# Recurrence in two slots a unit, with one feed-forward round between slots, on one core

## The chip, the cores and the metric

One NeuronCore of a Trainium2 chip runs the whole program. TensorE (PE) multiplies into PSUM, which has eight banks of 512 fp32 columns; VectorE (DVE) and ScalarE (ACT) take the results out of PSUM; GpSimd (POOL) does elementwise work on SBUF; SyncE (SP) issues DMAs. Each engine works through its own instructions in a fixed order and waits on semaphores. The metric is the device time of one execution in microseconds, the median of several runs.

## The reference, cut to what matters

```python
# r, k, v, w, a, b: (batch 4, heads 8, seq 768, dim 40)
for t in range(S):
    y[:, :, t] = einsum('bhd,bhde->bhe', r_t, state)
    Sa = einsum('bhde,bhe->bhd', state, a_t)
    state = state * w_t[:, :, None, :] - einsum('bhd,bhe->bhde', Sa, b_t)
    state = state + einsum('bhd,bhe->bhde', v_t, k_t)
x = y.transpose(0, 2, 1, 3).reshape(3072, 320)
h = x @ w_in                      # 320 -> 2048
g = h * clip(h + 3, 0, 6) / 6
out = g @ w_out                   # 2048 -> 320
```

A recurrence over 768 steps with a 40x40 state for each of 32 heads, then a feed-forward block over its 3072 output rows.

## The kernel before

**Units.** The sequence is cut into 12 blocks of 64 steps. A unit is one block of two batch entries: 24 units (`NK`), in 6 groups of four (`NU`). Within a unit the recurrence is turned into matrix products. What does not need the state is prepared ahead (`prepare`, stages W, gam, A, B, F, factor, K, E, EV): transposes of the inputs, decays by two scans on DVE (lines 541 and 552), score products of 64x64, and EV, a product with V. F of four units together gives a triangular matrix that DVE inverts (`invert`): some 60 small multiply and add instructions one after another (lines 738 and 744), then two stream transposes, tb and tt (lines 747 and 752). Two products on PE (`third_block`, lines 773 and 796) with four ACT copies after each finish the inverse, for two units at a time. What needs the state (`step`, stages RT, VT, R, C, S, U, UT, rS, sn, H, y, move, move2) follows unit by unit: R reads the state, U and UT need R (added to EV by DVE, line 857) and the inverse, H needs UT, y needs the masked H, and sn adds into the state. The moves are DMAs that lay y out as the feed-forward's input.

**Products in quarters.** Recurrence products use the array in four quarters, 64x64 each, and write pairs of PSUM banks: `ps_pair` deals a pair, and several products of up to 512 columns together share one. The weights of UT, rS and y are taken 64 columns wide (`SLOT`) although the data is 40 wide (`D`).

**Feed-forward.** Each unit has two rounds. A round is `expand` (32 full 128x128 matmul instructions as the trace counts them, line 1051, and 16 that are 64 rows deep, the `narrow` part), an ACT relu and a DVE multiply (lines 1066 and 1067) for each of two banks, and `contract` (16 instructions 320 columns wide, line 1092), which runs one round later. `feed_forward` is a generator that gives this in pieces: four pieces of `expand` and eight of `contract`.

**Order.** Everything is in an order written out by hand. The first two groups have tables of their own (lines 1131 to 1303), and after them 18 turns of inversion steps and 1.25 pieces of feed-forward each. From line 1307 on, each unit of the recurrence is cut into four blocks (`BLOCKS`); in each block `a_block` runs the stages of the unit in hand, then those of a unit four to six ahead, each as a run of products by `together`, and between those runs `feed` deals some 1.4 to 3.1 pieces of feed-forward with, while an inversion is open, two or three of its steps a piece. The recurrence ends well before the feed-forward: the last stretch is feed-forward alone.

**PSUM.** Two `pair` tiles and two one-bank `h` tiles for the feed-forward's hidden sums, one bank `one` for whole transposes and one, `o`, for the output.

The part of `together` by which a run's products come first and its results after the whole run:

```python
                rest = stage()
                next(rest)
                begun.append((name, rest))
```

Of the kernel before, what the change touches and what calls it, by code (L numbers as in the profile page):

```python
# [30 lines left out]
def kernel(  # L31
# [68 lines left out]
    lent = tc.tile_pool(name="lent", bufs=1, space=PSUM)  # L100
    pools = {"lent": lent.__enter__(), "pair": ps}
    pairs = deque([("pair", 2), ("pair", 2), ("lent", 1)])

    def pair():

        pairs.rotate(-1)
        tag, bufs = pairs[-1]
        return pools[tag].tile([P, 2, 512], F32, name=tag, tag=tag, bufs=bufs)

    def begun_ffn():  # L110

        lent.__exit__(None, None, None)
        pairs.clear()
        pairs.append(("pair", 2))
        pools["h"] = ctx.enter_context(tc.tile_pool(name="hidden", bufs=1, space=PSUM))


    def ps_any(shape):
        tag, bufs = ring[0]
        ring.rotate(-1)  # L120
        at = 0
        if tag == "whole":
            t = pair()
            open_half[0] = None
        elif tag != "pair":
            t = bank(tag, [P, 512], bufs)
        elif open_half[0] is None:
            t = open_half[0] = pair()
        else:
            t, at = open_half[0], 512  # L130
            open_half[0] = None
        views, step = [], 1
        for d in reversed(shape[1:]):
            views.insert(0, [step, d])
            step *= d
        return _ap(t[:], at, views)
# [3 lines left out]
    def ps_pair(*dims):  # L140
# [4 lines left out]
        if shared[0] is None or shared[1] + n > 512:  # L145
            shared[:] = pair(), 0
            open_half[0] = None
        at = shared[1]
# [5 lines left out]
        t = shared[0][:]  # L154
# [53 lines left out]
    nc.vector.memset(start[:], 0.0)  # L208
    nc.vector.memset(start[:].rearrange("p (n i) -> p n i", i=HB + 1)[:, :, 0:1], 1.0)
# [216 lines left out]
    PE, DONE = 1, 2  # L426
# [94 lines left out]
    def prepare(i, F):  # L521
        n, o = i % NU, data[i]
        halves = i >= 2 * NU
        def w_stage():
# [14 lines left out]
            fetch("W", following(i))  # L539
            prods = o["prods"] = tmp.tile([P, NB, 2, HB + 1], F32, name="prods", bufs=2)  # L540
# [5 lines left out]
        def gam_stage():  # L546
# [14 lines left out]
            def copy(to, x):  # L561
                if i < NU:
# [12 lines left out]
            if NU <= i <= 2 * NU:  # L575
                fetch("V", i)
# [57 lines left out]
        def factor_stage():  # L634
# [29 lines left out]
            if i > 2 * NU:  # L664
                fetch("V", i)
# [3 lines left out]
        def k_stage():  # L669
            x = turn_pairs(o["KN"])  # L670
            yield PE
            kt = o["kt"] = turned("kt")
            nc.vector.tensor_tensor(out=kt[:], in0=x[:], in1=o["rg"][:], op=ALU.mult)
# [143 lines left out]
    def step(i):  # L817
# [52 lines left out]
        def s_S():  # L870
# [10 lines left out]
            new_U()  # L881

        def s_U():

            if fresh:
                new_U()
# [16 lines left out]
        def s_UT():  # L903

            up = ps_pair(2, P)
            for j in range(2):
                for s in range(2):
                    for x in range(2):
                        for rs in range(2):
                            pr = 2 * j + rs  # L910
                            nc.tensor.matmul(out=up[x][half(rs), j, half(x ^ s)],
                                             lhsT=RR[half(x), s, pr * D:pr * D + SLOT],
# [7 lines left out]
        def s_rS():  # L920

            ysp = ps_pair(2, 2, BL)
            for j in range(2):
                for q in range(2):
                    for s in range(2):
                        for rs in range(2):
                            nc.tensor.matmul(out=ysp[rs][half(s), j, q, :],  # L927
                                             lhsT=m["S"][half(rs, D), q, j, half(s)],
# [32 lines left out]
        def s_y():  # L961
            y = ps_pair(NPR, BL)
            for name in "KB":
                for pr in range(NPR):
                    j, rs = pr // 2, pr % 2
                    for s in range(2):
                        for q in range(2):
                            h = 2 * pr + s
                            nc.tensor.matmul(  # L969
                                out=y[q][half(s), pr, :],  # L970
                                lhsT=o[name][half(q), h * D:h * D + SLOT],
# [44 lines left out]
    narrow, spread, LATEST = [], [False], 2  # L1016
# [7 lines left out]
    def feed_forward():  # L1024

        last = None
        while True:
# [7 lines left out]
            yield from expand(ready[i], r * NQ, gts)  # L1035
# [9 lines left out]
    def expand(xt, j0, gts):  # L1045

        hp = [pools["h"].tile([P, NQ, P], F32, name="h", tag="h", bufs=2) for _ in range(2)]
        begun = [0, 0]

        def add(c, i, lhsT, rhs):  # L1050
            nc.tensor.matmul(out=hp[c][:, i, :], lhsT=lhsT, rhs=rhs, start=(begun[c] == 0),  # L1051
# [11 lines left out]
        def results():  # L1063
            for c in range(2):
                gt = ffn.tile([P, NQ, P], F32, name="gt", bufs=5)
                nc.scalar.activation(out=gt[:], in_=hp[c][:], func=AF.Relu, bias=three[:], scale=1.0)  # L1066
                nc.vector.scalar_tensor_tensor(out=gt[:], in0=gt[:], scalar=6.0, in1=hp[c][:],  # L1067
                                               op0=ALU.min, op1=ALU.mult)
                gts.append(gt)

        narrow.append(short)
        for c in range(2):
# [53 lines left out]
    def pieces(n):  # L1126

        owed[0] += n * (8 / 9 if spread[0] else 1)
# [20 lines left out]
    def run(stage, steps=0, mixed=0, deals=0):  # L1149

        for at in stage:
            if at == DONE:
                return
            aside(steps, mixed)
            deal(deals)

# [143 lines left out]
    for _ in range(18):  # L1300
        aside(3)
        pieces(1.25)
    aside(3 * L)

    OWN_STAGES = [["RT", "VT"], ["R", "C", "S"], ["U", "UT", "rS"], ["sn", "H"], ["y"],
                  ["move", "move2"]]
    AHEAD_STAGES = [["W", "gam"], ["A", "B"], ["F", "K"], ["E", "factor"], ["EV"]]  # L1310
    CLOSE_STAGES = [["W", "gam"], ["A", "B"], ["F", "K", "factor"], ["E"], ["EV"]]


    PRODUCTS = ["W", "S", "K", "RT", "VT", "A", "B", "factor",
                "y", "EV", "R", "C", "U", "UT", "rS", "sn", "H", "E", "F"]
    RESULTS = ["RT", "y", "W", "VT", "EV", "R", "S", "C", "A", "B", "move", "move2",
               "U", "UT", "rS", "F", "K", "sn", "H", "E", "factor", "gam"]
    TURNS = PRODUCTS[:3]
    WIDTH = {"R": NPR * D, "U": NPR * D, "sn": NPR * D, "EV": NPR * D}
    BLOCKS = 4  # L1320
    FIRST_NARROW = PRODUCTS[len(TURNS)]

    def together(stages):

        begun, banks = [], 0

        def finish():
            begun.sort(key=lambda x: RESULTS.index(x[0]))
            for _, rest in begun:
                for _ in rest:  # L1330
                    pass
            begun.clear()
            shared[0] = open_half[0] = None
            ring.clear()
            ring.extend(TURNS_IN)

        for name in PRODUCTS:
            if name == FIRST_NARROW and narrow and spread[0] and stages:
                narrow[0]()
            for stage in stages.get(name, []):  # L1340
                if name in TURNS:
                    need = 2 * (open_half[0] is None) if ring[0][0] == "pair" else 1
                else:
                    width = WIDTH.get(name, NPR * BL)
                    need = 2 * (shared[0] is None or shared[1] + width > 512)
                if banks + need > 5:
                    finish()
                    banks, need = 0, 1 if name in TURNS else 2
                banks += need
                rest = stage()  # L1350
                next(rest)
                begun.append((name, rest))
        begun.extend((name, stage()) for name in stages if name not in PRODUCTS
                     for stage in stages[name])
        finish()

    begins = {u: max(3 * (u - 2 * NU), BLOCKS * (u - NU - AHEAD)) for u in range(2 * NU, NK)}
    coming, ahead, own = deque(range(2 * NU, NK)), {}, {}

    def a_block(m):  # L1360

        if coming and begins[coming[0]] == m:
            u = coming.popleft()
            close = coming and begins[coming[0]] < m + BLOCKS
            ahead[u, m] = prepared(u), CLOSE_STAGES if close else AHEAD_STAGES
        if m % BLOCKS == 0 and m // BLOCKS + NU < NK:
            i = m // BLOCKS + NU
            own[i, m] = step(i), OWN_STAGES
        parts = {}, {}
        for (u, begin), (fs, order) in sorted(own.items()) + sorted(ahead.items()):  # L1370
            if m - begin < len(order):
                for name in order[m - begin]:
                    parts[begin % BLOCKS > 0].setdefault(name, []).append(fs[name])
        for k, part in enumerate(parts):
            together(part)
            if any(u % NU == NU - 1 and m - begin == 2 and k == (begin % BLOCKS > 0)
                   for u, begin in ahead):
                third.clear()
                side.append(invert(group_F[-1], third))
            yield  # L1380

    def feed(n, inversion):

        whole = int(n)
        for k in range(whole):
            pieces(1)
            aside(inversion)
        pieces(n - whole)

    m = 0  # L1390
    for i in range(NU, NK):
        spread[0] = i >= 2 * NU - 1
        for j in range(BLOCKS):
            rate, inversion = 3.5, 0
            if i + AHEAD >= NK + NU - 1:
                rate = 4.5
            if i < 2 * NU - 1:
                rate = 2.8
            parts = a_block(m)
            next(parts)  # L1400
            if side or i % NU == NU - 1 and rate < 4:

                rate, inversion = 6.2, 2 + (i < 2 * NU)
            feed(rate / 2, inversion)
            for _ in parts:
                pass
            if i % NU < 2 and j < 2:
                if i % NU == 0:
# [43 lines left out]
```

## Time and profile before

| what | value |
|---|---|
| median of 3 runs | 799.55 us (799.53 to 800.25) |
| span of the profiled execution | 798.4 us |
| PE busy | 727.1 us, 91% |
| DVE busy | 501.3 us, 63% |
| ACT busy | 307.2 us, 38% |
| POOL busy | 176.3 us, 22% |
| PE busy in 300:700 | 398.5 of 400 us |
| PE busy in 0:140 | 81.4 of 140 us |

The profile is of one execution. Its tables give, for each group of instructions, the line of the kernel, the engine, what is written from what, the shape and the count, then total and mean time, then the engine's idle time just before them and what ended it. A matmul of fp32 stands in the trace as two instructions. Timelines give start, length, and the count of a merged run. Since matmuls are pipelined, the price of a run is read from its start to the next run's start.

### The profile page before, as it was taken

Reading aid. Unit: us, or ns where it says so; the run is one execution under the profiler, and the core shown is the slowest. Engines: PE = TensorE matmul, PEld = TensorE weight load, DVE = VectorE, ACT = ScalarE, POOL = GpSimd, SP = SyncE. Lnnn points to the kernel's source line nnn. Section 1 sums busy time; section 2 is a strip of 40 time slices with the busy share of each in tenths; the row PEclk is TensorE's granted clock in tenths of the full one; section 3 lists DMA queues with packets and bytes.
Section 4 is the critical chain, followed back from the end, with each engine's and each line's share of the span. In section 5 each row is a group of like instructions: output and inputs, shape, how many; then the busy total and the mean of one; then the engine's idle time right before and its main releaser. Section 6 shows DMA issues by size and latency. Waiting matters only on the chain.

```text
span 798.4 us, 35294 instructions
## 1 busy us (share of the span) xinstructions
PE 727.1 (91%) x15832; PEld 617.9 (77%) x15832; DVE 501.3 (63%) x986; ACT 307.2 (38%) x648; POOL 176.3 (22%) x318
## 2 busy tenths in 40 slices
PE   5624676999999989999999999999999999999998
PEld 4624575878778878888888888888888888888886
DVE  8889787679555699455698445898444983322210
ACT  2336653321654424453344453324444324412111
POOL 6403012420322222223124123304122202000000
PEclk9855888999999999999999999999999999999999
DMA  9484563420224321233222233213222101110000
GB/s 122 88 183 111 143 169 56 76 50 9 49 52 68 64 51 31 50 64 56 44 43 43 44 59 64 46 33 58 44 51 46 24 17 30 30 25 13 14 19 17
DMA packets 174214, 45.02 MB, mean 56 GB/s; under 512 B 157424, under 2 KB 172784, under 8 KB 174064
## 3 DMA queue, kind: packets, MB, share of 16 engines
q1 hardware_dynamic: 169760, 42.03, 27.6%
q8 instruction: 125, 2.05, 1.1%
q10 hardware_dynamic: 4304, 0.74, 0.6%
q14 instruction: 25, 0.20, 0.1%
HBM read 34.08 MB, written 3.93 MB: 48 GB/s over the span
## 4 chain that ended last, share of the span: by engine, by line
PE 73%; DVE 13%; issue 5%; SPq 3%; DMA 3%; ACT 2%; POOL 1%; DVEq 0%; POOLq 0%; ACTq 0%
PE h L1051 25%; PE o L1092 22%; PE pair L509 4%; PE pair L969 3%; PE pair L946 2%; DVE prod L738 2%; DVE x L744 2%; PE pair L481 2%; PE one L471 2%; SPq L455 2%; PE pair L853 2%; PE pair L891 2%; DVE prods L541 1%; PE pair L927 1%; DVE wm L552 1%
## 5 line engine op out<-in xcount | busy, mean ns | idle before, releaser
L1051 PE MATMUL h<-xt,win 128*128 128x128 f32 (+1 forms) x2304 | 251.3, 283 | 2.7 <-DVE gt L1067 2.7
L1051 PEld LDWEIGHTS h<-xt,win 128*128 128x128 f32 (+1 forms) x2304 | 231.8, 193 | 19.8 <-issue 4.4
L1092 PE MATMUL o<-wout,gt 128*128 128x320 f32 x768 | 229.6, 442 | 0.0
L1092 PEld LDWEIGHTS o<-wout,gt 128*128 128x128 f32 x768 | 138.1, 190 | 50.4 <-issue 0.2
L1067 DVE SCALAR_TENSOR_TENSOR gt<-gt,h 128x512 f32<-128x512 f32 x96 | 62.0, 681 | 70.5 <-ACT gt L1066 70.5
L1066 ACT ACTIVATE gt<-h,three 128x512 f32<-128x512 f32 x96 | 62.2, 686 | 99.7 <-PE h L1051 99.3
L981 POOL TENSOR_TENSOR yg<-ys,gam 128x512 f32<-128x512 f32 x22 | 39.0, 1772 | 160.3 <-DVE ys L980 73.7
L738 DVE TENSOR_TENSOR prod<-x 128x30 f32<-128x30 f32 (+9 forms) x180 | 67.1, 373 | 8.8 <-POOL x L723 3.3
L660 POOL TENSOR_TENSOR KBt<-K,rgt 128x320 f32<-128x320 f32 x22 | 19.0, 865 | 212.6 <-ACT rgt L649 197.2
L744 DVE TENSOR_TENSOR x<-x,prod 128x30 f32<-128x30 f32 (+9 forms) x180 | 62.2, 345 | 5.4
L954 DVE TENSOR_TENSOR state<-pair,state 40x320 f32<-40x320 f32 (+1 forms) x44 | 21.4, 487 | 65.4 <-PE pair L946 39.1
L517 DVE COPY_PREDICATED score<-mask,pair 128x512 f32<-128x512 int32 x71 | 50.0, 723 | 1.0 <-PE pair L509 0.5
L980 DVE TENSOR_TENSOR ys<-pair,ys 128x512 f32<-128x512 f32 x22 | 15.2, 690 | 40.8 <-PE pair L687 21.8
L552 DVE TENSOR_TENSOR_SCAN wm<-wm,start 128x528 f32<-128x528 f32 x24 | 37.8, 1574 | 0.8
L541 DVE TENSOR_TENSOR_SCAN prods<-wm,start 128x528 f32<-128x528 f32 x24 | 30.8, 1288 | 10.1 <-ACT wm L538 10.0
L831 ACT ACTIVATE RT<-pair 128x512 f32<-128x512 f32 x21 | 12.5, 597 | 52.8 <-PE pair L481 52.8
L692 ACT ACTIVATE EV<-pair 64x320 f32<-64x320 f32 x44 | 19.0, 432 | 32.9 <-PE pair L687 22.3
L806 ACT ACTIVATE tinv<-pair 32x256 f32<-32x256 f32 x48 | 18.0, 375 | 30.8 <-PE pair L796 30.1
L569 POOL COPY gam<-prods 128x256 f32<-128x256 f32 x24 | 22.5, 938 | 31.4 <-DVE prods L541 30.6
L969 PE MATMUL pair<-score,KBt 64*64 64x64 f32 x1472 | 27.8, 224 | 1.2 <-DVE state L954 1.2
L1110 ACT ACTIVATE ob<-o 128x320 f32<-128x320 f32 x22 | 9.6, 435 | 49.0 <-PE o L1092 24.8
L969 PEld LDWEIGHTS pair<-score,KBt 64*64 64x64 f32 x1472 | 24.5, 137 | 3.8 <-DVE state L954 1.8
(262 smaller groups left out, 1049.0 us busy)
## 6 DMA issues: line engine op xcount, KB each, us to landing
V<-in_v_dram SPq DMA_DIRECT2D x96, 40.0 KB
out_dram<-ob SPq DMA_DIRECT2D x47, 80.0 KB
R<-in_r_dram SPq DMA_DIRECT2D x92, 40.0 KB
B<-in_b_dram SPq DMA_DIRECT2D x42, 80.0 KB
K<-in_k_dram SPq DMA_DIRECT2D x42, 80.0 KB
W<-in_w_dram SPq DMA_DIRECT2D x37, 80.0 KB
A<-in_a_dram SPq DMA_DIRECT2D x37, 80.0 KB
xt<-yg SPq DMA_DIRECT2D x72, 40.0 KB
```

The costliest lines, as they stand in the source:

```text
L509: nc.tensor.matmul(out=o[i][half(q), n, :], lhsT=lhs[half(i, D), n ^ (2 * q * swap), half(q)], rhs=rhs[half(i, D), n, half(q)], start=True ...
L517: nc.vector.copy_predicated(out=x[:].rearrange("p (i h) t -> p i h t", i=2), mask=mask8, data=o[2])
L541: nc.vector.tensor_tensor_scan(out=prods[:].rearrange("p r m i -> p (r m i)"), data0=wm[:, 0:SCAN], data1=start[:], initial=0.0, op0=ALU.m ...
L552: nc.vector.tensor_tensor_scan(out=back, data0=back, data1=start[:], initial=0.0, op0=ALU.mult, op1=ALU.add)
L738: nc.vector.tensor_tensor(out=pv, in0=_ap(x[:], (i + 1) * L + i, [[L, n], [0, i]]), in1=_ap(x[:], i * L, [[0, n], [1, i]]), op=ALU.mult,)
L744: nc.vector.tensor_tensor(out=rest, in0=rest, in1=pv, op=ALU.add)
L969: nc.tensor.matmul(out=y[q][half(s), pr, :], lhsT=o[name][half(q), h * D:h * D + SLOT], rhs=m[name][half(q), 4 * rs + 2 * s + j, :], start ...
L981: nc.gpsimd.tensor_tensor(out=yg[:], in0=m["ys"][:].rearrange("p r q t -> p r (q t)"), in1=o["G"][:], op=ALU.mult)
L1051: nc.tensor.matmul(out=hp[c][:, i, :], lhsT=lhsT, rhs=rhs, start=(begun[c] == 0), stop=(begun[c] == 3 * NQ - 1))
L1066: nc.scalar.activation(out=gt[:], in_=hp[c][:], func=AF.Relu, bias=three[:], scale=1.0)
L1067: nc.vector.scalar_tensor_tensor(out=gt[:], in0=gt[:], scalar=6.0, in1=hp[c][:], op0=ALU.min, op1=ALU.mult)
L1092: nc.tensor.matmul(out=op[:], lhsT=gts[c][:, n, :], rhs=wout[:, c * HJ + r * NQ + n, :], start=((split or r == 0) and c == 0 and n == 0), ...
```

## The change

The steady part, from the second group's recurrence and the third group's preparation on, is ordered anew. Each unit has two slots. The even slot of unit i holds, of the units in hand, RT and VT of unit i and rS, sn, H, y of unit i-1, and of unit i+4 the stages F, E and factor. The odd slot holds R, C, S, U, UT of unit i, W, gam, A, B, K of unit i+5, and EV of unit i+4. A slot's products stand in one run, with results taken between them (`both`), and the `narrow` part of the next round of feed-forward ends the run. Between two slots stands a `window`: one whole round (expand and the contract of the round before), and two rounds in every eighth slot. A window in which no unit is ready for the feed-forward is empty. Inversion steps go two to a piece into the windows, four to a piece in the first two.

PSUM pairs become three fixed tiles, given out by longest free; `expand` takes one of them for its hidden sums. The six banks are written once by PE at the start. UT, rS and y take weights of 40 columns. K is transposed in halves like A and B, and two copies of `gam_stage` move from DVE to ACT for units from the third group on. The 18 turns of filler ahead of the steady part are gone.

```diff
+    pairs = [[ps.tile([P, 2, 512], F32, name=f"pair{i}"), i] for i in range(3)]
     def pair():
-        pairs.rotate(-1)
-        tag, bufs = pairs[-1]
-        return pools[tag].tile([P, 2, 512], F32, name=tag, tag=tag, bufs=bufs)
+        x = min(pairs, key=lambda x: x[1])
+        clock[0] += 1
+        x[1] = HELD + clock[0]
+        taken.append(x)
+        return x[0]
...
     nc.vector.memset(start[:], 0.0)
+    for x in pairs:
+        for c in range(2):
+            nc.tensor.matmul(out=x[0][:, c, :], lhsT=start[:, 0:P], rhs=start[:, 0:512], start=True, stop=True)
     nc.vector.memset(start[:].rearrange("p (n i) -> p n i", i=HB + 1)[:, :, 0:1], 1.0)
...
             def copy(to, x):
-                if i < NU:
+                if i < NU or halves:
                     nc.scalar.activation(out=to, in_=x, func=AF.Copy)
...
         def k_stage():
-            x = turn_pairs(o["KN"])
+            x = turn_in(o["KN"], halves)
...
-                            nc.tensor.matmul(out=up[x][half(rs), j, half(x ^ s)],
-                                             lhsT=RR[half(x), s, pr * D:pr * D + SLOT],
+                            nc.tensor.matmul(out=up[x][half(rs, D), j, half(x ^ s)],
+                                             lhsT=RR[half(x), s, pr * D:pr * D + D],
...
-                                lhsT=o[name][half(q), h * D:h * D + SLOT],
+                                lhsT=o[name][half(q), h * D:h * D + D],
...
-    for _ in range(18):
-        aside(3)
-        pieces(1.25)
-    aside(3 * L)
...
+        results("move", "move2")
+        if s % 2:
+            products("W")
+            results("W", once=True)
+            both("R", "EV")
+            both("C")
+            results("W")
+            both("U", "UT")
+            products("A", "B")
+            products("K")
+            if narrow:
+                narrow[0]()
+            both("S")
+            results("gam", "A", "B", "K")
+        else:
+            both("F")
+            both("H", "E")
+            both("rS", "sn")
+            both("y")
+            both("RT", "VT")
+            both("factor")
+            if narrow:
+                narrow[0]()
...
+    for s in range(begins(2 * NU), 2 * NK + 2):
+        if s == begins(2 * NU):
+            spread[0] = True
+            while next(stream) != OPEN:
+                pass
+            lends_hidden()
+        slot(s)
+        window(s, 2 if s % (2 * NU) == 2 * NU - 1 and s > 2 * NU else 1)
```

`both(names)` writes the products of the named stages and then at once the instructions that take their results; `products` and `results` do the one or the other. `window` draws pieces of feed-forward until the next round opens, and in the first and third slot of a group it also runs the two `third_block`s: their first product after the sixth piece, or at the end where there are fewer, and the second at the end.

## The prediction

> **What bounds the kernel now.** I read the page's busy times and slices first, then the timelines of PE and DVE, then the groups of ACT and DVE.
>
> ```profile
> PE 727.1 (91%) x15832; PEld 617.9 (77%) x15832; DVE 501.3 (63%) x986; ACT 307.2 (38%) x648; POOL 176.3 (22%) x318
> PE   5624676999999989999999999999999999999998
> PEclk9855888999999999999999999999999999999999
> ```
>
> After the first seventh PE is busy to the end. Waits of PE that I find from 176 us on, longer than 0.25 us, come to 8.9 us (2.0 up to 240, 4.4 up to 300, 2.5 after). So the change gains what it takes off PE's own work, and loses each wait that the new order puts into it. The last 60 us are feed-forward alone: no chain of the recurrence binds now.
>
> What PE's work costs is read from start to start:
>
> ```profile
> 405.68 0.60 PE L875 MATMUL one<-ident,state 128*128 128x128 f32 x4
> 406.21 1.16 PE L1051 MATMUL h<-xt,win 64*128 64x128 f32 x16
> 407.21 0.41 PE L481 MATMUL pair<-ident,A 64*128 64x64 f32 x8
> 407.45 0.42 PE L481 MATMUL pair<-ident,B 64*128 64x64 f32 x8
> 407.79 0.68 PE L853 MATMUL pair<-state,at 40*64 40x40 f32 x32
> 408.28 0.67 PE L509 MATMUL pair<-RT,VT 40*64 40x64 f32 x32
> 408.89 2.94 PE L1051 MATMUL h<-xt,win 128*128 128x128 f32 x24
> 411.67 0.70 PE L1092 MATMUL o<-wout,gt 128*128 128x320 f32 x2
> ```
>
> L853 takes 0.49 up to L509, which is of the same 64x64 kind; L509 takes 0.61 up to L1051. Leaving a quartered run costs 0.12; inside one, going from product to product costs nothing. A whole 128x128 instruction is 0.111 (24 in 2.78, 0.1 of it the change to L1092), one of L1092 0.269.
>
> **Part by part: PE's own work.** From 176.2 us on, the program order of before changes its kind of run 379 times, that of after 277 times. Priced by kind (0.05 between halves and quarters, 0.10 to 0.12 out of quarters, 0.1 to 0.2 into them) this is 40.8 against 32.9: **-7.9**. K in halves: eight at 0.035 for four at 0.107 with one switch, 0.15 for each of 16 units: **-2.4**. Weights of 40 columns: UT, rS and y have 128 of the trace's instructions a unit, 20 units. With 64-column weights one costs 15.2 ns whether 40 (L853) or 64 columns stream; 40-column weights with 40 streaming, L946, cost 10.3. No row has 40 with 64 streaming. Above, the gain is 4.9 ns each, 12.6 us; below, none. A whole-array L1051 is 111 ns for 128 columns, so 64 in four quarters need 13.9 by streaming alone. I take that: 1.3 ns each, **-3.4**.
>
> The Trainium skill (TensorE: Matmul & The Clock Gate, section LDWEIGHTS) says that a weight load takes time by its columns alone. By that an instruction here would fall to 40/64 of 15.2, and the term would be an estimated -14.6; L946's 10.3 is near, but streams fewer columns.
>
> **Waits at the start.** Six matmuls 512 columns wide are put ahead of all others. From L1092, at two instructions each, one is 0.86 at the full rate, and early transposes here take about twice as long as later ones (four in 1.09 against 0.60): 5.2 to 10.3 us from 1.7 us on. DVE's next memset waits for them, and after it the zeroing that the first copies need; those copies began at 5.5. DVE is 82% busy over the first 40 us (32.8 us of the two windows), and waits 2.8 for a weight DMA at 39, which absorbs part. Below 0, above 9: I take **+3.5**.
>
> **Waits in the slots.** These are walked with the following rows; a result starts 0.27 after its last product, and a product 0.06 after its result.
>
> ```profile
> L517 DVE COPY_PREDICATED score<-mask,pair 128x512 f32<-128x512 int32 x71 | 50.0, 723 | 1.0 <-PE pair L509 0.5
> L552 DVE TENSOR_TENSOR_SCAN wm<-wm,start 128x528 f32<-128x528 f32 x24 | 37.8, 1574 | 0.8
> L541 DVE TENSOR_TENSOR_SCAN prods<-wm,start 128x528 f32<-128x528 f32 x24 | 30.8, 1288 | 10.1 <-ACT wm L538 10.0
> ```
>
> ```profile
> L630 ACT ACTIVATE F<-pair 32x256 f32<-32x256 f32 x64 | 20.6, 368 | 0.4
> L781 ACT ACTIVATE zs<-pair 32x256 f32<-32x256 f32 x40 | 15.0, 375 | 9.1 <-PE pair L773 8.7
> ```
>
> Odd slot, PE from 0: W 0.53, R, EV, C to 1.96, U and UT to 2.94, A, B, K to 3.83, narrow to 4.8, S to 5.4. R's add is done at 1.76, ahead of U. It has no wait. But DVE masks C until 2.94, scans (1.29), inverts a row (0.25), scans (1.57), ACT copies twice (0.82), and only then at, bt, kt follow at 0.68 each: bt is ready at 8.4.
>
> Even slot: F, H, E, rS, sn to 2.6; y uses F's banks, and F's six ACT copies of 0.368 end at 2.95, so y waits 0.4. With narrow 0.45 for a slot, some 14 slots: **+6.3**. Eight late odd slots have only C between R and U, 0.3 each: **+2.4**. All of these can vanish or double.
>
> *Empty windows.* In five places (slots 11, 17, 25, 33, 41) no window follows the odd slot. PE has no narrow there and is done at 4.4; F needs bt at 8.4. Four of them wait 4.1, the last, without units ahead, 0.5: **+16.9**. Before, feed-forward pieces stood there.
>
> *Third blocks.* In five windows (slots 10, 18, 26, ...) the two third-block products now stand with nothing between. After `expand` ACT has two relus of 0.69, then four copies of L781: the second product waits 2.55, and four times ACT's lateness costs 0.7 in the next slot: **+15.5**.
>
> *Inversions.* DVE's order, as before:
>
> ```profile
> 177.83 0.35 DVE L744 TENSOR_TENSOR x<-x,prod 128x184 f32<-128x184 f32 x1
> ...
> 197.56 1.98 DVE L747 STREAM_TRANSPOSE tb<-x 128x1024 f32<-128x1024 f32 x1
> 199.40 2.03 DVE L752 STREAM_TRANSPOSE tt<-x 128x1024 f32<-128x1024 f32 x1
> 202.44 0.69 DVE L1067 SCALAR_TENSOR_TENSOR gt<-gt,h 128x512 f32<-128x512 f32 x1 [1.01 <-ACT gt L1066]
> ```
>
> The first inversion of the steady part runs here at about 0.42 us a step beside whole rounds on PE. In after the filler's steps are gone from its place: at the step of 177.83 DVE stands before slot 7's scans, whose W is transposed on PE only at about 185.5. DVE is through with bt and kt at 193; 36 steps and one round's gt follow (15.7), and only then the mask of slot 8's E, at 208.8. The narrow products of slot 8 take E's banks, and PE is there at 198.5: a wait of **+11**. Later inversions put 36 steps (14.4) and two rounds' gt (2.6) on DVE after an odd slot's chain (9.1): DVE is free at 26.1 where PE's next even slot starts at 22.5. There y waits for H's mask, 1.4 more than above, and narrow 0.35 (four times, **+7**). In its window tb is ready 2.9 after PE reaches line 773 (four times, **+11.6**).
>
> These sum to 70.7; the 8.9 of the old order's own waits go. No row of before shows one of the new waits; each is worked out from the lengths of its chain. The first inversion, the empty windows and half of the third blocks alone make 35, my lower end; with the small ones doubled and half as much again for the inversions I come to 95, the upper.
>
> **Clock.** Idle PE costs rate here:
>
> ```profile
> 117.00:121.00 4.00, 1.22 (x11) 1.00 1.01 248
> 121.00:128.00 7.00, 3.75 (x22) 0.52 0.13 22
> ```
>
> A gap of 6.0 us (to 124.25) brought 7 us at half rate; one of 2.1 at 109.5 brought none. I count the wait of 11 alone: half of 7, **+3.4**; 0 below, 17 if all five waits over 4 us cost the same. The Trainium skill (TensorE: Matmul & The Clock Gate, Part 1, the HAM clock gate) puts the drop after one idle window of about 3.4 us, on a free-running clock. That rule speaks against this change: by it the waits of 4.1 us could each lose an estimated 1.7, and the sum would be 6.8 higher.
>
> **The sum** against the profiled execution: 798.4 - 7.9 - 2.4 - 3.4 + 3.5 + 70.7 - 8.9 + 3.4 = 853.4. The median of the runs is 1.15 above the span, so 854.5; I say **854**.
>
> **Rivals.** *Faster.* PE's own work decides: the results come ahead of the products that need them, since DVE is idle 37% and ACT 62%. Then the work falls by 13.7 (22.9 at 10.3 ns), the old waits of 8.9 go, 3.5 is added: 780, with a few short waits 785. For it speaks that the old order held PE at 99.6% in 300:700; against it, that it did so with feed-forward between each product and its consumer, which the new slots have not. It decides from where all waits together stay under 19 us: the first inversion and half of the empty windows alone make that. *Half.* Only the coarse waits show (35 to 45, and 2 for the clock): 817 to 828 by the same sum. Then the walks' smaller terms are wrong. *Worse.* The clock drops at every 4 us wait (13.6 more) and the slots' small waits double (8.7 more): 877. *The change does not do what it says*: its runs are no fewer. The program order excludes this.
>
> **Chances.** Forecast (832 to 872) 0.50; half (803 to 832) 0.22; worse 0.10; faster 0.15; between, within 0.2%, 0.03. (0.2%, 1.6 us, is about what a measurement of this kernel can tell from no change.) Faster by more 0.15, same 0.03, slower 0.82. The range takes in forecast, nearly all of half and most of worse: 806 to 880.
>
> **What would show it.** In the new profile PE should have a wait of about 11 us near 200 on DVE's mask; four of some 4 us on `bt`; five of 2.5 before the second third-block product, four of 3 on tb; and y in even slots waiting on ACT's F. UT, rS and y should fall from 15.2 to about 14 ns an instruction. The recurrence should last to within some 30 us of the end. PE busy for the whole after 200 us would make the prediction wrong; so would DVE doing the first inversion's steps ahead of slot 7's scans.

## The result and the profile after

931.85 us (928.74 to 936.4, four runs) against 799.9 before: ratio 1.167, 95% interval 1.162 to 1.172. The profiled execution spans 934.7 us, 136.3 more than before. The direction was forecast, the size was not: 854 was said, with 880 as the upper end.

One correction to what stands above: a round's contract is dealt in four pieces of two matmuls each (four instructions of the trace), not in eight; a round has eight pieces in all.

Busy time, PE's slices and the granted clock, from the page of the changed kernel:

```profile
PE 777.5 (83%) x15908; PEld 657.6 (70%) x15908; DVE 493.5 (53%) x954; ACT 324.3 (35%) x680; POOL 166.3 (18%) x318
PE   5637769876979998799898799898789898799978
PEclk8856789996968998889999889999789999799999
```

Where before has nines from the first seventh on, PE now falls to 6 to 8 in every group, and the clock falls with it. The waits of PE from 176 us on (us in total, times, longest):

```profile
PE pair L795 <- DVE tb L769: 13.5, 4, 3.4
PE pair L641 <- DVE bt L614: 11.7, 4, 2.9
PE pair L818 <- ACT zs L803: 10.3, 10, 1.8
PE pair L1081 <- DVE score L536: 9.4, 1, 9.4
PE pair L1081 <- DMA xt<-yg: 6.1, 1, 6.1
PE pair L966 <- issue: 6.0, 4, 1.9
PE pair L989 <- issue: 5.6, 7, 1.9
PE pair L500 <- issue: 4.4, 7, 1.2
```

In this program line 641 is F's first product, 795 and 818 are the third block's two, 1081 is expand, 966 is sn, 989 is y, and 500 transposes. The four rows with tb, bt, zs and the score of 9.4 are the waits that the prediction named: 13.5, 11.7, 10.3 and 9.4, where it had 11.6, 16.9, 15.5 and 11. "issue" means that PE waited for nothing that the profile shows. Idle time in the whole list is 97.0 us, against 6.7 before; 19.3 of it is issue and 9.7 is DMA.

What one wait does to what follows (timeline of PE, start and duration):

```profile
378.53 0.65 PE L897 MATMUL one<-ident,state 128*128 128x128 f32 x4
382.13 1.13 PE L641 MATMUL pair<-bt,at 40*64 40x64 f32 x32 [2.94 <-DVE bt L614]
383.01 1.10 PE L528 MATMUL pair<-RT,UT 40*64 40x64 f32 x32
...
445.23 0.65 PE L528 MATMUL pair<-RT,UT 40*64 40x64 f32 x32
445.69 0.65 PE L528 MATMUL pair<-at,kt 40*64 40x64 f32 x32
```

This is an empty window. After a wait of 2.94 us, 32 instructions of line 528 take 0.85 from start to start; the same ones at 445 take 0.46. The windows (stretch, length, PE busy with its instructions, granted clock, then DMA) show that this holds for one half of a group's slots and not for the other:

```profile
345.00:405.00 60.00, 49.02 (x1268) 0.81 0.22 42
405.00:485.00 80.00, 75.13 (x1346) 1.00 0.22 40
485.00:545.00 60.00, 47.33 (x1306) 0.86 0.22 42
```

**The account.** I take every PE instruction from its start to the start of the next. Its kind's price at full rate is work, an excess of over 0.25 us a wait, what the half rate adds a term of its own, and the rest are changes of kind. From 176 us on, in us:

| | before | after | difference | predicted |
|---|---|---|---|---|
| work at the old prices | 565.7 | 565.8 | 0 | 0 |
| changes of kind, K in halves, 40 columns | 43.4 | 19.5 | -23.9 | -13.7 |
| waits (in the forecast, the later start too) | 8.9 | 120.6 | +111.7 | +65.3 |
| half rate | 0 | 48.1 | +48.1 | +3.4 |

The differences come to 135.9, the spans differ by 136.3. The 120.6 is more than the 97.0 of the list above because it is read from start to start, and a matmul's end in the trace lies about 0.2 us behind the start of the next run (445.23 + 0.65 against 445.69). Where a wait ends and the half rate begins is a matter of how such an account is cut, by some us. A bound that does not depend on it: the record of the granted clock has 129.7 us at half rate after 176 us, in 20 stretches, so that the half rate cost 65 us at most, less what PE waited inside them. The same account is used for each experiment below.

### The profile page after: what moved, and what is told of

It reads as the page before. It is cut to its first block, busy times and chain, and to the rows that moved or that the text cites. A ratio compares the mean times of both kernels' runs of the same rounds, so it can differ in the third digit from the quotient of the medians.

```text
span 934.7 us, 35378 instructions
## 1 busy us (share of the span) xinstructions
PE 777.5 (83%) x15908; PEld 657.6 (70%) x15908; DVE 493.5 (53%) x954; ACT 324.3 (35%) x680; POOL 166.3 (18%) x318
## 4 chain that ended last, share of the span: by engine, by line
PE 46%; DVE 17%; ACT 5%; issue 5%; DMA 1%; SPq 1%; POOL 0%; DVEq 0%; ACTq 0%; POOLq 0%
PE pair L1081 17%; PE o L1124 14%; DVE prod L760 4%; DVE x L766 4%; DVE gt L1097 3%; PE pair L989 2%; ACT gt L1096 2%; PE pair L500 2%; PE pair L528 2%; PE pair L966 1%; PE pair L641 1%; PE pair L911 1%; DVE wm L573 1%; DVE prods L562 1%; PE pair L931 1%
## 5 line engine op out<-in xcount | busy, mean ns | idle before, releaser
L1081 PE MATMUL pair<-xt,win 128*128 128x128 f32 (+1 forms) x2304 | 252.0, 290 | 21.4 <-DVE score L536 9.4
L1081 PEld LDWEIGHTS pair<-xt,win 128*128 128x128 f32 (+1 forms) x2304 | 238.1, 202 | 31.8 <-issue 10.8
L1097 DVE SCALAR_TENSOR_TENSOR gt<-gt,pair 128x512 f32<-128x512 f32 x96 | 66.0, 687 | 167.8 <-ACT gt L1096 167.8
L1096 ACT ACTIVATE gt<-pair,three 128x512 f32<-128x512 f32 x96 | 65.9, 687 | 233.4 <-PE pair L1081 182.8
L1001 POOL TENSOR_TENSOR yg<-ys,gam 128x512 f32<-128x512 f32 x22 | 28.3, 1288 | 398.6 <-DVE ys L1000 330.9
L879 DVE TENSOR_TENSOR RR<-pair,EV 128x320 f32<-128x320 f32 x22 | 10.8, 489 | 80.7 <-PE pair L709 64.9
L989 PE MATMUL pair<-score,KBt 64*40 64x64 f32 x1536 | 36.7, 247 | 10.6 <-issue 6.4
L989 PEld LDWEIGHTS pair<-score,KBt 64*40 64x40 f32 x1536 | 30.5, 134 | 15.3 <-issue 9.1
L795 PE MATMUL pair<-tb,F 32*32 32x32 f32 x768 | 10.0, 202 | 27.0 <-DVE tb L769 26.9
L709 PE MATMUL pair<-V,score 64*64 64x40 f32 x768 | 19.7, 247 | 11.5 <-issue 4.4
```

Of the source, the lines that this page charges most:

```text
L989: nc.tensor.matmul(out=y[q][half(s, D), pr, :], lhsT=o[name][half(q), h * D:h * D + D], rhs=m[name][half(q), 4 * rs + 2 * s + j, :], start ...
L1001: nc.gpsimd.tensor_tensor(out=yg[:], in0=m["ys"][:].rearrange("p r q t -> p r (q t)"), in1=o["G"][:], op=ALU.mult)
L1096: nc.scalar.activation(out=gt[:], in_=hp[c], func=AF.Relu, bias=three[:], scale=1.0)
```

## Experiments

Theory A: PE waits for results, since no feed-forward stands between a product and its consumer, as predicted. Theory B: each such wait costs again through the clock. Theory C: long runs of small products outrun the supply of instructions. Rival: the products themselves became dearer. The trace of the changed kernel speaks against the rival at once: from start to start at the full clock, an instruction of expand takes 111.7 ns in both kernels, and one of the scores (line 509, now 528) 14.5 where it took 15.2.

**1. Unread matmuls in the waits.**

```diff
+    def warm(n):
+        if n:
+            t = bank("one", [P, 512], 1)
+            for _ in range(n):
+                nc.tensor.matmul(out=t[:], lhsT=ident[:], rhs=win2[:, 0:512], start=True, stop=True)
...
```

> The changed kernel with 52 extra matmuls of 128x128 by 128x512, whose results nobody reads, put on PE just ahead of the products that wait longest (ten in slot 8, three before the first third-block product of each group and two between its last two, three in each empty window, one before y after each inversion). By the rows of a 128x320 instruction (0.269 us, two a matmul) one takes 0.86 us, 45 us in all, which lie inside waits of about 45 us. Theory B (the waits cost their own length and then stretches at half the granted clock): the waits become busy time of the same length, the clock stays up behind them, and of the 48 us that the half rate cost from 176 us on 30 to 45 go: 887 to 902 us. Theory A (dependency waits alone, the low clock being only how the throttle answers to products of 64x64): 930 to 940, with the same slices below 9 in the row of the granted clock. Rival, that small products in long runs pull the clock down by themselves: drops stay in the slots although no wait stands before them, 925 to 940.

908.8 us, ratio to before 1.135 (1.132 to 1.139). By the account the half rate falls from 48.1 to 6.2 and the waits by 39.4; the new matmuls put 49.0 of work and 4.6 of changes in their place. The same stretches as above, in this kernel:

```profile
345.00:405.00 60.00, 54.65 (x1302) 0.97 0.25 48
485.00:545.00 60.00, 55.31 (x1319) 1.00 0.24 45
```

The slots hold the same small products and run at the full clock once no long pause stands among them. So 42 of the 48 us are the price of the waits that were filled, and B is shown. The 81 us of waits that stay, most of them shorter, cost 6.2. The time lies above B's 887 to 902 because the filling was some 10 us longer than the waits that it covered.

**2. Small products alone.** The program leaves out the whole computation and writes zeros: runs of `quarters(768, columns, streams)` between whole matmuls.

> No recurrence and no feed-forward: zeros are written to the output, and PE runs quartered products of zeros that wait for nothing. Four runs of 768 products (1536 instructions in the trace) with weights of 64, 40, 64, 40 columns and 64, 64, 40, 40 streamed columns, between whole-array matmuls of 13.8 us each; then eight times 96 products of 64 by 64 and four whole matmuls. Theory C (instructions come in 16 KB packets, one for some 127 matmul instructions, and long runs of small products outrun them): idle time put down to issue inside the four long runs, of about 1 us for each packet, and none or nearly none in the mixed part, where the whole matmuls give 3.4 us for the next packet. Without C: no such idle time, 1536 instructions in 23.3 us (15.2 ns each) for 64 columns. Price of a 40-column weight with 64 streamed: 14.0 ns an instruction (21.5 us for the run without gaps) if streaming sets it, 10.3 ns (15.8 us) if columns set it; 64 columns with 40 streamed 15.2; 40 with 40 10.3.

310 us. The first run in the timeline of PE:

```profile
17.00 3.02 PE L73 MATMUL pair<-x 64*64 64x64 f32 x191
21.42 2.09 PE L73 MATMUL pair<-x 64*64 64x64 f32 x128 [1.39 <-issue]
25.14 2.09 PE L73 MATMUL pair<-x 64*64 64x64 f32 x128 [1.64 <-issue]
28.60 2.09 PE L73 MATMUL pair<-x 64*64 64x64 f32 x128 [1.36 <-issue]
```

191 instructions run without a gap (159 to 255 in the other three runs), and then 128 come every 3.5 to 4.0 us, whatever their columns: 27 to 31 ns an instruction in place of 14.9. 128 matmul instructions with their 128 weight loads are one packet of 16 KB on the instruction queue (12 packets in the trace from 17 to 60 us). Issue idle is 68.7 us in all. In the mixed part three gaps of about 1 us remain, where I expected none or nearly none. C is shown, and sharper than expected: gaps of mostly 1.4 to 2.0 us where I had 1. In the changed kernel it looks like this:

```profile
446.61 0.43 PE L966 MATMUL pair<-V,KBt 64*40 64x40 f32 x25
448.43 0.24 PE L966 MATMUL pair<-V,KBt 64*40 64x40 f32 x4 [1.40 <-issue]
```

A 16 KB packet began at 445.8 and took 1.2 us; PE stops inside a stage, between two products of one kind. Inside the stretches without gaps of experiment 2 an instruction takes 14.9 ns with weights of 64 columns and 64 streamed, 14.2 with 40 and 64, 14.8 with 64 and 40, and 9.7 with 40 and 40: the larger of the two sets it, nearly.

**3. The filler put back.**

```diff
+    for _ in range(18):
+        aside(3)
+        pieces(1.25)
+    aside(3 * L)
```

> The changed kernel with the old order's 18 filler turns (three inversion steps and 1.25 feed-forward pieces each) put back ahead of slot 7. The step that was missed in slot 8, a wait of 9.7 us for the mask and 17 us at half rate behind it (8.5 us), should go. Theory A: 922 if only the wait goes; with B 914. The 22 pieces (2.8 rounds) that are used up here are missed later: if each gives another empty window (3.1 us of wait and some 3 at half rate), 10 to 17 of this come back and the time is 920 to 932. Rival, that the first inversion sits on the path wherever it stands: 932 or more.

930.8, ratio 1.162 (1.158 to 1.167): no change. The wait of 9.4 is gone, but the waits on bt and V grow by 3.4, those on zs by 1.4, and the half rate by 5.2. F waits for bt five times instead of four, as it would if the rounds were only spent earlier.

**4. Contract pieces dealt into the slots.**

```diff
+            piece()
             both("C")
             results("W")
+            piece()
             both("U", "UT")
+            piece()
             products("A", "B")
...
```

and likewise three in the even slot.

> The changed kernel with the second half of a round (four contract pieces of 0.55 us) taken out of the window and dealt into the next slot, one piece between two runs of products, wherever the window has no third blocks. Work and number of rounds are the same; some 100 more switches at 0.2 us add up to 15 to 20 us. Theory C and A (bare runs of dependent small products wait for results and for instructions): the issue waits (25) and the small waits for gt, RR, score and F (some 20) mostly go, and with them, by B, the drops of the clock in the slots: 850 to 890. If the drops come only from the long waits of empty windows and third blocks, which stay here, 900 to 920. Rival, that only PE's own work became dearer: 945 to 955.

911.2, ratio 1.138 (1.134 to 1.142): the second case, in which the drops hang on the long waits that stay. Waits fall by 37.9 (issue idle from 19.3 to 8.0, DMA from 9.7 to 1.3) and half rate by 11.7, but changes of kind rise by 23.2, nearly all that the change had saved there. The four groups of long waits are as they were.

**5. The third block's products apart.**

```diff
-                if k == 6 and n is not None:
+                if k == (6 if n == 0 else 2) and n is not None and n >= 0:
```

> The changed kernel with contract pieces dealt into the slots, and besides, in the five windows that hold both products of a third block, the first of them moved forward by two expand pieces (1.8 us of PE's work between the two). Theory A: the second product's wait for the four copies (10.8 us in the run before this) falls to some 2, so 9 less than 911: 902. With B also the stretch at half rate behind each of five: 895 to 900. Rival, that the first product now waits for tb or for a bank instead: 911.

901.4, ratio 1.128 (1.126 to 1.129), on top of experiment 4: A's 902, and not the 895 to 900 of A and B together. By the account waits fall by 7.6 (zs from 10.8 to 1.3, with new ones for gt and a DMA) and half rate by 6.8; work and changes of kind take 4.6 of that back.

**6. Pauses of known length.** This program, too, leaves out the whole computation and writes zeros.

```diff
+def pause(n):
+    for _ in range(n):
+        nc.scalar.activation(out=y[:], in_=wide[:], func=AF.Copy)
+    nc.tensor.matmul(out=wide[:], lhsT=x[:, 0:P], rhs=y[:], start=True, stop=True)
```

> No recurrence and no feed-forward, zeros to no output but the last copy: PE alternates 13 to 16 whole matmuls of 128x512 with a pause made by one to nine dependent copies on ACT (0.7 us each: pauses of about 1.0, 1.7, 2.4, 3.1, 3.8, 5.2 and 6.6 us), four times each; then pauses of 1.0 to 3.1 us with 48 products of 64x64 (1.4 us) on either side. Theory B as the changed kernel's trace suggests it: between whole matmuls no drop up to 1.7, some at 2.4 and 3.1, one each time from 5.2 on, each costing 3.4 to 6.8 us at half rate; between small products drops already at 1.7 to 2.4. If the slots' drops have another cause than the pauses, the second part is like the first. The Trainium skill (TensorE: Matmul & The Clock Gate, Part 1) has a free-running window of about 3.4 us that must be idle as a whole, so by it no pause under 3.4 us would bring a drop in either part.

Drops in four pauses each, counted in the record of the granted clock:

| pause, us | 0.75 | 1.38 | 2.00 | 2.63 | 3.26 | 4.52 | 5.77 |
|---|---|---|---|---|---|---|---|
| between whole matmuls | 0 | 0 | 1 | 1 | 3 | 4 | 4 |
| beside small products | 0 | 0 | 3 | 4 | | | |

Each drop lasted 3.41 or 6.83 us. Read by itself, the table says that pauses of 2.0 to 2.6 us, which bring a drop in two cases of eight between whole matmuls, bring one in seven of eight beside small products. But the record of the clock has another reason for that. All 20 drops begin a whole number of times 3.413 us apart, so the clock is set on fixed intervals of that length, and where a pause falls on them decides. Here are the intervals around three pauses of 2.00 us: one between whole matmuls, with a drop; one beside small products, with a drop; and the fourth beside small products, without:

```profile
152.99:156.41 3.42, 1.42 (x4) 1.00 0.00 0
156.41:159.82 3.41, 3.41 (x5) 0.50 0.00 0
```

```profile
699.13:702.55 3.42, 1.42 (x3) 1.00 0.00 0
702.55:705.96 3.41, 3.41 (x90) 0.50 0.02 5
719.61:723.02 3.41, 2.36 (x94) 1.00 0.02 5
723.02:726.43 3.41, 2.45 (x96) 1.00 0.01 2
```

Each of the first two pauses lies within one interval, which leaves PE 1.42 us of work in it; the third is cut in two by the end of an interval. This holds for all 44 pauses: in the 20 with a drop at least 2.00 us fell into one interval, in the 24 without at most 1.88. So the small products are not needed to explain any case here; three of the four pauses of 2.0 beside them happened to lie in one interval, and one of the four between whole matmuls. The Trainium skill (TensorE: Matmul & The Clock Gate, Part 1) gives a free-running window of about 3.4 us, which the fixed intervals agree with, and warns there of idle gaps over about 3.4 us; drops after 2.0 us differ from that. In the changed kernel the line is less sharp: drops follow intervals with up to 2.2 us of busy PE in 3.41 (2.12 ahead of the drop at 293.08). Why that is so, no run here shows.

**7. 40-column weights alone, in the old order; fixed pairs in strict rotation.** The edits of UT, rS and y are those of the diff above.

```diff
+    fixed = [ps.tile([P, 2, 512], F32, name=f"pair{i}") for i in range(3)]
...
     def pair():
         pairs.rotate(-1)
...
+        return pairs[-1]
...
+        hp = [fixed[2][:, c].rearrange("p (n t) -> p n t", t=P) for c in range(2)]
```

> The kernel before, in its own order, with the one part of the change that takes nothing away from the order: weights of 40 columns for UT, rS and y (2560 of the trace's instructions in 20 units), which needs PSUM pairs that are allotted once; they are zeroed at the start by six short bf16 matmuls between 2.4 and 5.0 us, ahead of the first transposes. In the runs of zeros without waits an instruction of 64 by 64 columns took 14.9 ns and one of 40-column weights with 64 streamed 14.2; in the changed kernel's rS it was 14.0 against 15.2 in the order of before. If streaming bounds them, 0.7 to 1.3 ns each: 1.8 to 3.4 us faster, ratio 0.9957 to 0.998. If columns alone did, 12.6 us faster, 0.984. Rival, that the fixed pairs bring new waits between PE and the copies out of PSUM (before took any free one of a pool): the same or slower.

827.9, ratio 1.036 (1.033 to 1.038): the rival. Waits rise by 21.8. Line 795 here, the third block's second product, waits 8.9 for bt, whose pair it is given, and feed-forward waits 7.4 for its own product.

**8. The same with K in halves.**

> As the last one, and K transposed in halves like A and B, in a run with them: 16 times eight instructions at 0.035 us with no change of kind for four at 0.107 with one switch of 0.15, 2.4 us by the rows of before. 4.2 to 5.8 us faster than the kernel before, ratio 0.9927 to 0.9947, if both work; no more than the last one if K's pair of PSUM banks, which it now takes where it took one bank, splits a group of runs in two (0.2 to 0.3 us of switches each).

858.1, ratio 1.074 (1.072 to 1.077). F's product now waits for kt, 12 times and 18.2 us: K's sums hold a pair that F needs. The list of the changed kernel has no wait of F for kt; it has a third pair and gives pairs out by release. Which of the two hides it was not tried, nor whether the 2.4 us can be had alone with the pairs of experiment 9.

**9. The same as 7, the pair released first, hidden sums in two tiles** (`+` marks what differs from 7).

```diff
...
+    x = min(pairs, key=lambda x: x[1])
...
+        hp = [pools["h"].tile([P, NQ, P], F32, name="h", tag="h", bufs=2) for _ in range(2)]
```

> The kernel before with 40-column weights for UT, rS and y once more, now without the two things that came along with the fixed PSUM pairs in the first try (the third block's product waiting for bt, 8.9 us, because strict rotation gave it the pair of A and B; feed-forward's second relu waiting for DVE, because both halves of the hidden sums lay in one tile): of two fixed pairs the one released first is taken, and the hidden sums have two tiles of one bank as before. If those two waits and the clock they cost were the 28 us of the first try, the ratio comes back to 0.996 to 1.001 (1.8 to 3.4 us gained on PE; the zeroing at the start cost up to 2.3 us there). If it stays at 1.03, the 40-column weights or the fixed pairs themselves cost it.

796.5 against 799.9, ratio 0.9956 (0.9937 to 0.9975): faster than both kernels. PE's row and its largest wait after 176 us:

```profile
PE 728.0 (91%) x15838; PEld 616.3 (77%) x15838; DVE 500.3 (63%) x986; ACT 305.9 (38%) x648; POOL 176.6 (22%) x318
```

```profile
PE pair L706 <- DVE wm L601: 2.4, 2, 1.4
```

The clock drops only in the last 0.3 us. The account gives 3.3 for the weights, where the prediction had 3.4. Inside a run, from start to start, an instruction of UT falls from 15.0 to 13.6 ns, one of rS from 13.9 to 13.6 and one of y from 15.2 to 14.1, which is 2.5 us for the 2560 of them.

**10. Both relus ahead of both products.** Experiment 7 had pointed at the hidden sums' tile, and the changed kernel has the same (timeline of ACT):

```profile
410.90 0.69 ACT L1096 ACTIVATE gt<-pair,three 128x512 f32<-128x512 f32 x1 [2.30 <-PE pair L1081]
412.34 0.69 ACT L1096 ACTIVATE gt<-pair,three 128x512 f32<-128x512 f32 x1 [0.75 <-DVE gt L1097]
```

ACT's second relu waits for DVE's product of the other half, in the same two-bank tile.

```diff
             for c in range(2):
                 nc.scalar.activation(out=gt[:], in_=hp[c], func=AF.Relu, ...)
+                gts.append(gt)
+            for c in range(2):
+                gt = gts[c]
                 nc.vector.scalar_tensor_tensor(out=gt[:], in0=gt[:], ...)
```

> The changed kernel with feed-forward's four results in another order of issue: both relus on ACT, then both products on DVE. In the changed kernel ACT's second relu stands 0.75 us behind DVE's first product (50.7 us idle in 96), which before it did not. If that lateness of ACT counts (the second third-block product waits for copies behind the relus, and F's copies stand behind them), each of ten such waits falls by 0.7 and some drops of the clock go: 2 to 10 us less, 922 to 930. If only the end of the four counts, which stays at four times 0.7, no change: 932.

914.7, ratio 1.141 (1.136 to 1.146): 17 us faster, where I expected 2 to 10. ACT's 50.7 us of idle time behind DVE are gone; the waits fall by 13.3 (zs from 10.3 to 7.0), the half rate by 10.4.

**11. One round in every window.**

```diff
-        window(s, 2 if s % (2 * NU) == 2 * NU - 1 and s > 2 * NU else 1)
+        window(s, 1)
```

> The changed kernel with one round in every window, also in those ahead of an inversion, which hold two. Three of the four empty windows that wait then have a round (9 us of waits less, some 7 at half rate); but of the inversion's steps 16 more stand, with nothing beside them, ahead of its end: 6.7 us on DVE, four times, in the wait for tb. Theory A, both counted: 930 to 950. If the inversion's steps go beside PE's work anyway, 915.

920.6, ratio 1.151 (1.147 to 1.154), between the two forecasts. The wait for tb grows from 13.5 to 38.8 and that for bt falls from 11.7 to 2.9; the waits together grow by 3.2. Still it is faster, since half rate costs 26.6 in place of 48.1: fewer and longer waits (14 low stretches of 97.4 us in all, instead of 20 of 129.7) cost less clock here than many short ones.

**12. The covers together:** experiments 4, 5 and 10 and 40 unread matmuls.

> The changed kernel with its waits covered together: contract pieces dealt into the slots, the first third-block product two pieces earlier, both relus ahead of both products, and 40 unread matmuls of 0.86 us in slot 8, in the empty windows and ahead of the first third-block product. By A the waits of 9.6, 11.7 and 13.8 us turn into 34 us of busy time, no gain: 895 to 900. By B the stretches at half rate behind them go too (of 36 us that were left with the pieces dealt, some 25 to 30): 865 to 878. If it stays above 895, the clock has another cause than the waits.

881.2, ratio 1.100 (1.097 to 1.104), 3 us above the range of B and well below that of A. Waits are 44.1, half rate 11.8, changes of kind 43.7, and 33 of work are the unread matmuls. By this account the rest over before is all waits, clock and filling; PE's own work with its changes of kind, 43.7 here and 43.4 before, is no dearer.

## Why the prediction was wrong, step by step

The clock, at 48.1 for 3.4, and the waits, at 111.7 for 65.3, each missed by some 45 us. Either error alone would have carried the time past the range's end of 880; PE's own work gave 10 back.

- **PE's own work**, "-7.9", "-2.4", "-3.4": right in sign, 23.9 for 13.7. The weights' 3.4 came out at 2.5 to 3.3 (experiment 9), and streaming sets it where 64 columns stream, as I took it (14.9 to 14.2 ns in experiment 2). But "15.2 ns" held for y alone; rS was at 13.9 before the change. The rest of the excess is put down to changes of kind: in the two traces the run changes among whole, half, quartered and 32x32 products 293 and 170 times after 176.2 us, 123 fewer, where I had counted 102 fewer in the program order.
- **The start**, "+3.5": the last wait of the second group's preparation, on PE, begins 4.5 us later, and ends 5.4 later (178.93 instead of 173.51).
- **The named waits**: first inversion 9.4 for 11; empty windows 11.7 for 16.9; third blocks 10.3 for 15.5; tb 13.5 for 11.6. Walks of chains from the old rows' lengths held to about a third, at the named places. The small ones in the slots were named wrongly: y's wait on F, forecast at 6.3 with narrow's, is 1.3 in all, while waits for RR, gt and masks, which the walk held to be free, make most of 23.1 where 15.7 were forecast.
- **Waits not named.** The walk of a slot had only results in it. It did not have instructions: the slots' runs of some 180 to 280 small instructions go faster than their packets come (19.3 idle, experiment 2). Nor DMA: 9.7, with 6.1 at the very end, where the last round waits for its input. Nor that fixed pairs put both hidden sums into one tile: "two relus of 0.69, then four copies" are in truth relu, product, relu, product, and experiment 10 prices it at 17 us with its clock.
- **Clock: the step that failed most.** "I count the wait of 11 alone ... +3.4; 0 below, 17 if all five waits over 4 us cost the same." It was 48. I had two rows, a gap of 6.0 us with a drop and one of 2.1 without, and read a threshold between them; both ends of my bounds stood on that. The trace of before held two more rows, which speak against it. PE waits 2.83 us up to 86.30, and 2.07 and 0.99 up to 95.65 and 97.79, and the clock drops after both:

```profile
86.30 0.50 PE L946 MATMUL pair<-V,KBt 64*64 64x40 f32 x20 [2.83 <-issue]
95.65 0.33 PE L911 MATMUL lent<-tinv,RR 64*64 64x64 f32 x5 [2.07 <-issue]
97.79 1.09 PE L853 MATMUL pair<-state,at 40*64 40x40 f32 x32 [0.99 <-ACT U L895]
```

```profile
83.77:87.18 3.41, 0.88 (x60) 1.00 0.60 164
87.18:90.59 3.41, 3.41 (x97) 0.50 0.50 78
94.01:97.42 3.41, 1.03 (x37) 1.00 0.38 82
97.42:104.25 6.83, 6.46 (x58) 0.50 0.48 116
```

That the gap of 2.1 brought no drop was no rule: on the same intervals it is cut at 111.07 into 1.6 and 0.5 us. The changed kernel has waits of 1.5 to 3.5 us all along. By experiment 6's line of 2 us in one interval, the waits that I had walked myself (one of 11, four of 4.1, four of 2.9, five of 2.55) would have brought some ten or eleven drops, an estimated 18 to 36 us at 1.7 to 3.4 each.

- **Rivals.** "Worse", 877, had the right mechanism and stopped at the waits of 4 us. "Faster" was right that the work falls, and about the condition: it decides where all waits stay under 19 us, and they are six times that.

What stays open: why the clock drops in the changed kernel after less idle time in an interval than in experiment 6, and how much of the 112 us of waits each cause would cost alone, since taking one away moves the next (experiments 3 and 11).

## What to carry to other kernels

A pause of 2 us on PE can cost more than 2 us. In experiment 6 the clock dropped when some 2 us of idle time fell into one of its intervals of 3.41 us, and each drop cost up to half of 3.41 to 6.83 us. Worked out from that line, a pause of 2.0 us has an estimated chance of two in five, and one of 4.1 us is sure to bring a drop, wherever it falls. So count pauses, not only their sum, and read every drop in the trace with the waits ahead of it before taking a threshold from one row. Feed-forward pieces dealt between runs of small products look like costly switches (here 24 us of them), but they hide the results' latency, give the instruction supply time and hold the clock. Of a change with many parts, try the parts that leave the order alone by themselves: here one of them, 40-column weights, was worth about its predicted 3.4 us once the pairs were dealt by release and the hidden sums had two tiles (experiment 9); with neither it came out 28 us slower (experiment 7), and the two were not tried apart.

## What the runs showed of the hardware that I had not expected

- The clock is set on fixed intervals of 3.413 us, and in experiment 6 some 2 us of idle time in one of them brought a drop: at least 2.00 in 20 pauses with a drop, at most 1.88 in 24 without.
- The supply of instructions can bound PE: after the first 159 to 255 small matmul instructions of a run, 128 every 3.5 to 4.0 us, for all four sizes of product (experiment 2). The same instructions in batches of 192 with 3.7 us of whole matmuls between them ran nearly without gaps.
- In the run of 40 by 40 columns, where 128 instructions are 1.2 us of work at the full rate in every 3.5 to 4.0, the page shows the clock at 5 for five slices of 7.7 us in a row: gaps of the supply alone are enough to keep it low. In the first run, with 1.9 us of work in the same time, the page has it at 9 throughout.
- ACT's read of one bank waits for DVE's read of the neighbouring bank when both lie in one tile (0.75 us in the lines of experiment 10), and does not when they are two tiles (experiment 9 against 7: no idle time of the relus behind DVE against 65.3 us). The profile shows it as a wait of ACT on DVE; these runs don't tell whether the chip would need it.
